# One list of steps, sums on GpSimd and a weighed minus plane in a fused attention and dense layer

## The chip, the cores and the metric

The kernel runs on one core of one Trainium2 chip. A core has TensorE (matrix products, results in PSUM), VectorE (DVE in the profile), ScalarE (ACT), GpSimd (POOL), SyncE (SP, which here only issues DMAs) and 16 DMA engines. The metric is the device time of one execution in microseconds. PSUM has eight banks of 128 partitions x 512 fp32 numbers.

## The reference

The input x has 2048 rows of 512 numbers. A layernorm gives xn, and the result is x plus an attention branch plus a dense branch, both fed by xn, all in bf16:

```python
def _A_ref(x, wqkv, w_phi, wo):                    # H = 32 heads of Dh = 16
    q, k, v = ...                                  # x @ wqkv, split into heads
    pq = jnp.einsum("bhsd,hdf->bhsf", q, w_phi)
    pk = jnp.einsum("bhsd,hdf->bhsf", k, w_phi)
    phi_q = jnp.concatenate([softmax(pq), softmax(-pq)], axis=-1)
    phi_k = jnp.concatenate([softmax(pk), softmax(-pk)], axis=-1)
    kv = jnp.einsum("bhsf,bhsd->bhfd", phi_k, v)
    z  = jnp.einsum("bhsf->bhf", phi_k)
    num = jnp.einsum("bhqf,bhfd->bhqd", phi_q, kv)
    den = jnp.einsum("bhqf,bhf->bhq", phi_q, z)[..., None] + 1e-6
    return (num / den, heads joined) @ wo

def _B_ref(x, w1, b1, w2):                         # 512 -> 1792 -> 512
    h = jnp.einsum("bsd,df->bsf", x, w1) + b1
    return jnp.einsum("bsf,fd->bsd", mish(h), w2)

return x + _A_ref(xn, ...) + _B_ref(xn, ...)
```

## The kernel before, in words

The 2048 rows are 16 tiles of 128, four tiles to a group. The softmax features are worked on in eight steps s: s = 0 to 3 are the keys of groups 0 to 3, s = 4 to 7 the queries. The key weights and w_phi are multiplied into one matrix `wkp` at the start (`fold`), the query weights into `wqp` later.

**Keys.** `logits` is a product of xnT (xn transposed) with `wkp`, copied out of PSUM to `p_sb`. `extremes` makes two planes per group on VectorE: logits minus their maximum over the 16 features of a head, and minimum minus logits, by a tree of maxima or minima (L234, L240) and a subtraction (L245). `exponentials` raises both on ScalarE, `normalise` (L277 sum, L287 reciprocal, L288 copy, L292 product) makes softmaxes of them on VectorE, and `accumulate` multiplies with the values (`value`, in `vext` with a column of ones), summing kv and z over all 16 tiles in `pkv` (L304). `mask_kv` keeps each head's own block, as `kvm`.

**Queries.** Here the exponentials are not normalised. Each tile of them is transposed by a DMA (`turn`, into `qT`), and `attend` multiplies it with `kvm` in 32 products of 32 rows and 36 columns, four of which lie side by side in TensorE's rows (`tile_position`, L350). Plus and minus planes, each with its own numerator, denominator and softmax sum, come out apart in `pnd`; ScalarE copies them to `ds` and `nm` (L359, L362), and `combine` joins them on VectorE (L379 to L403), a DMA transposes the result into `ob`, and `project_out` adds the product with `wo` to the same PSUM bank, `po`, as the dense branch's second layer (`second_layer`, L422; L431). `residual` adds x, `store` issues the stores.

**Dense.** `hidden` makes 56 units of 128 features x 512 rows (4 products of 128x512 each, L194), `activate` applies Mish on ScalarE (L207).

**Layernorm.** `ln_stats` (L133, L135) runs on VectorE, the root on GpSimd; `ln_apply` on VectorE for group 1 and on GpSimd for groups 2 and 3 (L145). Group 0 is transposed on TensorE, the others by DMAs (`ln_turn_dma`, L163).

Nothing is scheduled by a tool: each engine works through its instructions in the order in which the program issues them, and waits where data or a buffer is missing. All DMAs but a few stand in SyncE's queue. The program first issues x (three loads of SyncE's, L450, L456, L459), the key weights, `wv` (L457) and w1 (L458); w2 (L556) and `wo` (L557) are issued behind the first two transposes of `xnT`. The order of the rest is written out by hand: a loop over s for the keys, in which the hidden units fill TensorE's time, then a straight list of calls for the queries.

Of the kernel before, what the change touches and what calls it, by code (L numbers as in the profile page):

```python
# [14 lines left out]
AX = mybir.AxisListType  # L15


@with_exitstack
def kernel(
# [41 lines left out]
    ps = ctx.enter_context(tc.tile_pool(name="ps", bufs=4, space=PSUM))  # L61
    upper = ExitStack()
    px = upper.enter_context(tc.tile_pool(name="px", bufs=1, space=PSUM))
    turns = [cycle([px, ps, ps, ps, ps])]

    def bank(name, dtype=FP32, pool=None):
        pool = pool or next(turns[0])
        return pool.tile([P, 512], dtype, name=name, tag="mm")

    def three_banks(name, bufs):  # L70
        stack = ExitStack()
        return stack, stack.enter_context(tc.tile_pool(name=name, bufs=bufs, space=PSUM))
# [4 lines left out]
    kvm = persist.tile([P, 8, 36], BF16, name="kvm")  # L77
# [17 lines left out]
    vext = [vpool.tile([P, TPG, 4, 4, 36], BF16, name=f"vext{i}") for i in range(2)]  # L95
# [11 lines left out]
    def fold(wT, dst, dve, kts=range(KT)):  # L107

        for kt in kts:
            pf = bank("pfold")  # L110
            for j in range(4):
                nc.tensor.matmul(  # L112
                    pf[:, j * P : (j + 1) * P],
                    lhsT=wT[:, j, kt * P : (kt + 1) * P],
                    rhs=Wbd[:, j, :],
                    start=True,
                    stop=True,
                )
            copy = nc.vector.tensor_copy if kt in dve else nc.scalar.copy
            copy(  # L120
                dst[:, kt, :].rearrange("p (b a c) -> p a b c", b=8, a=2),
                pf[:].rearrange("p (a b c) -> p a b c", a=2, b=8),
            )

    def ln_stats(t0, n, between=None):

        stats = lnp.tile([P, TPG, nc.vector.BN_STATS_DIM], FP32, name="stats")
        mv = lnp.tile([P, TPG, nc.vector.BN_AGGR_DIM], FP32, name="mv")
        rstd = lnp.tile([P, TPG], FP32, name="rstd")
        for i in range(n):  # L130
            if i == 1 and between is not None:
                between()
            nc.vector.bn_stats(stats[:, i, :], x_sb[:, t0 + i, :])  # L133
        for i in range(n):
            nc.vector.bn_aggr(mv[:, i, :], stats[:, i, :])  # L135
        nc.gpsimd.tensor_scalar(
            out=rstd[:, 0:n], in0=mv[:, 0:n, 1], scalar1=1e-5, scalar2=None, op0=ALU.add
        )
        nc.gpsimd.tensor_tensor(out=rstd[:, 0:n], in0=rstd[:, 0:n], in1=mhalf[:, 0:n], op=ALU.pow)
        return mv, rstd  # L140

    def ln_apply(t0, n, mv, rstd, xn, at):
        engine = nc.gpsimd if t0 > TPG else nc.vector
        for i in range(n):
            engine.tensor_scalar(  # L145
                out=xn[:, at + i, :],
                in0=x_sb[:, t0 + i, :],
                scalar1=mv[:, i, 0:1],
                scalar2=rstd[:, i : i + 1],
                op0=ALU.subtract,  # L150
                op1=ALU.mult,
            )

    def ln_turn_pe(t, xn, i, copy):
        ptr = bank("ptr", BF16)
        for kt in range(KT):
            nc.tensor.transpose(  # L157
                ptr[:, kt * P : (kt + 1) * P], xn[:, i, kt * P : (kt + 1) * P], ident[:]
            )
        copy(xnT[:, t, :, :], ptr[:].rearrange("p (k c) -> p k c", k=KT))  # L160

    def ln_turn_dma(t, xn, i):
        nc.sync.dma_start_transpose(  # L163
            out=xnT[:, t : t + 2, :, :].rearrange("p t k c -> p (t k) c"),
            in_=xn[:, i : i + 2, :].rearrange("p t c -> p (t c)"),
        )
# [12 lines left out]
    def value(t, copy):  # L179
        pv = project(wv, t)  # L180
        copy(
            vext[(t // TPG) % 2][:, t % TPG, :, :, 0:32].rearrange("p j r c -> p (j r) c"),
            pv.rearrange("p (j c) -> p j c", j=16),
        )

    units = iter([(g, f) for g in range(NG) for f in range(FT)])

    def hidden(n, pool=None, late=None):

        for _ in range(n):  # L190
            g, f = next(units)
            ph = bank("ph", FP32, pool)
            for kt in range(KT):
                nc.tensor.matmul(  # L194
                    ph[:],
                    lhsT=w1_sb[:, kt, f * P : (f + 1) * P],
                    rhs=xnT[:, g * TPG : (g + 1) * TPG, kt, :],
                    start=(kt == 0),
                    stop=(kt == KT - 1),
                )  # L200
            if late is None:
                activate(g, f, ph)
            else:
                late.append((g, f, ph))
# [7 lines left out]
    p_of, e_of, qT_of = {}, {}, {}  # L212

    def logits(s, i, copy):
        if i == 0:
            p_of[s] = smx.tile(
                [P, TPG, 512], BF16, name="p_sb" if s < 7 else "p_last", bufs=1
            )
        pp = project(wkp if s < NG else wqp, (s % NG) * TPG + i)
        copy(p_of[s][:, i, :], pp)  # L220

    def extremes(s, between=None, halves=(slice(0, TPG),)):

        if s not in e_of:
            e_of[s] = epool.tile([P, TPG, 16, 2, 32], BF16, name="e")
        for q in halves:
            n = q.stop - q.start
            e = e_of[s][:, q]
            pv = p_of[s][:, q, :].rearrange("p t (c e) -> p (t c) e", e=16)
            for pl, op in enumerate((ALU.max, ALU.min)):  # L230
                src = pv
                for half in (8, 4, 2):
                    m = smx.tile([P, 128, half], BF16, name=f"m{half}", bufs=1)[:, 0 : n * 32, :]
                    nc.vector.tensor_tensor(  # L234
                        out=m, in0=src[:, :, 0:half], in1=src[:, :, half : 2 * half], op=op
                    )
                    src = m

                m = smx.tile([P, 128, 1, 2], BF16, name="m1", bufs=1)[:, 0 : n * 32]
                nc.vector.tensor_tensor(out=m[:, :, 0, :], in0=src, in1=src[:, :, ::-1], op=op)  # L240
                if pl == 0 and between is not None:
                    between()
                mb = m.rearrange("p (b h) u o -> p b h u o", h=2).to_broadcast([P, n * 16, 2, 8, 2])
                p5 = pv.rearrange("p (b h) (e o) -> p b h e o", h=2, o=2)
                nc.vector.tensor_tensor(  # L245
                    out=e[:, :, :, pl, :].rearrange("p t b (h e o) -> p (t b) h e o", h=2, o=2),
                    in0=p5 if pl == 0 else mb,
                    in1=mb if pl == 0 else p5,
                    op=ALU.subtract,
                )  # L250

    def exponentials(s, ks=(0, 1)):
        for k in ks:
            m = 1 if s >= NG or (s > 1 and k == 0) else 2
            for i in range(2 * k, 2 * k + 2, m):
                v = e_of[s][:, i : i + m].rearrange("p t b l c -> p (t b l c)")
                nc.scalar.activation(v, v, ACT.Exp)  # L257
                if s >= NG:
                    turn(s, k, i)

    def turn(s, k, i):

        h = 2 * (s - NG) + k
        if i == 2 * k:
            qT_of[h] = epool.tile([P, 2, 8, P], BF16, name="qT", bufs=3)
        nc.sync.dma_start_transpose(
            out=qT_of[h][:, i - 2 * k, :, :],
            in_=e_of[s][:, i].rearrange("p b l c -> p (b l c)"),
        )

    def normalise(s, k, between=None):

        v = e_of[s][:, 2 * k : 2 * k + 2].rearrange("p t b l c -> p (t b l c)")
        t = smx.tile([P, 128], FP32, name="s")
        n = 64 if s > 1 and k == 0 else 128
        for c in range(0, 128, n):
            nc.vector.reduce_sum(  # L277
                t[:, c : c + n],
                v[:, 16 * c : 16 * c + 16 * n].rearrange("p (c e) -> p c e", e=16),
                axis=AX.X,  # L280
            )
        if between is not None:
            between()
        r = smx.tile([P, 128], BF16, name="r")
        r2 = smx.tile([P, 128, 2], BF16, name="r2")
        with nc.allow_low_precision("the softmaxes are bf16"):
            nc.vector.reciprocal(r[:], t[:])  # L287
# [8 lines left out]
    kv_of = {}  # L296

    def accumulate(g, pk):
        if g == 0:
            kv_of[0] = pk.tile([P, 8, 128], FP32, name="pkv", tag="kv")  # L300
        e = e_of.pop(g)
        for b in range(8):
            for i in range(TPG):
                nc.tensor.matmul(  # L304
                    kv_of[0][:, b, 0:66],
# [429 lines left out]
```

## Time and profile before

| | |
|---|---|
| time, median of 3 runs | 178.31 us (178.26 to 178.38) |
| span of the profiled execution, first to last instruction | 176.1 us; its own time isn't given apart from the three runs', and 2.2 us of their median lie around the span |
| granted TensorE clock | 1.000 |
| TensorE's last product ends | 172.2 us |
| GpSimd, largest row | L145 apply, 16.6 us in 8 instructions of 2.08 us |
| ScalarE, table loads | 13 of 1.28 us |

In the profile PE is TensorE's products, PEld its weight loads, SPq SyncE's issues of DMAs; a row of the timeline gives start, length, engine, line, operation, output <- input and count. The lengths of single products overlap (379 ns each at a rate of 216 ns), so rates are taken from the chain.

### The profile page before, as it was taken

The numbers are of one execution on the slowest core, as the hardware profiler recorded it, in microseconds if no ns is written. First come the engines' busy times: TensorE is split into PE (matmuls) and PEld (weight loads), VectorE is DVE, ScalarE is ACT, GpSimd is POOL, SyncE is SP. The second block draws the span as 40 slices with busy tenths as digits, with TensorE's granted clock in tenths as the row PEclk, the third lists the DMA queues.
The fourth block names the chain that finished last, engine by engine and source line by source line (L and its number), as shares of the span: only waits on it lengthen the run. The fifth ranks groups of instructions, "written<-read, shape, count | busy, mean of one in ns | idle before, by whom it ended". The sixth has DMA issues, their size and how long they took to land.

```text
span 176.1 us, 3589 instructions
## 1 busy us (share of the span) xinstructions
PE 171.1 (97%) x1422; PEld 81.6 (46%) x1422; DVE 154.1 (88%) x308; ACT 125.4 (71%) x176; POOL 28.5 (16%) x40
## 2 busy tenths in 40 slices
PE   6899999999999999999999999999999999999993
PEld 2444444454444545554454444444444444444561
DVE  0989999999999999999999979798789978789953
ACT  3667999999998899989996699489223863544200
POOL 4203039700799400000000000000000000000000
PEclk9999999999999999999999999999999999999999
DMA  5998895330023600000000942919945098394434
GB/s 139 272 416 314 131 348 177 60 61 4 0 49 69 124 0 0 0 0 4 0 0 0 179 92 56 100 29 133 229 119 93 3 170 99 91 121 123 65 89 149
DMA packets 44557, 18.08 MB, mean 103 GB/s; under 512 B 36988, under 2 KB 44028, under 8 KB 44540
## 3 DMA queue, kind: packets, MB, share of 16 engines
q1 hardware_dynamic: 43568, 17.50, 46.6%
q10 hardware_dynamic: 972, 0.35, 0.7%
q8 instruction: 11, 0.18, 0.4%
q14 instruction: 6, 0.05, 0.1%
HBM read 6.84 MB, written 2.10 MB: 51 GB/s over the span
## 4 chain that ended last, share of the span: by engine, by line
PE 93%; DVE 3%; DMA 2%; DVEq 0%; issue 0%
PE po L422 28%; PE ph L194 28%; PE pproj L173 22%; PE po L431 7%; PE pnd L350 3%; PE pkv L304 2%; DMA x_sb<-in_A_x_dram 2%; PE pwide L173 1%; DVE stats L499 1%; DVE x_sb L439 1%; PE pfold L112 1%; DVE xn L512 0%; DVE wkp L120 0%; DVE mv L503 0%; PE ptr L157 0%; DVEq L730 0%
## 5 line engine op out<-in xcount | busy, mean ns | idle before, releaser
L422 PE MATMUL po<-w_sb,acts 128*128 128x512 bf16 (+1 forms) x238 | 51.0, 367 | 0.0
L194 PE MATMUL ph<-xnT,w_sb 128*128 128x512 bf16 x224 | 49.5, 379 | 0.0
L207 ACT ACTIVATE acts<-ph,b1f 128x512 bf16<-128x512 f32 x56 | 34.6, 704 | 2.0 <-PE ph L194 1.9
L257 ACT ACTIVATE e<-e 128x1024 bf16<-128x1024 bf16 (+1 forms) x26 | 31.0, 1250 | 4.6 <-DVE e L245 4.6
L194 PEld LDWEIGHTS <-w_sb 128*128 128x128 bf16 x224 | 21.9, 98 | 26.4 <-issue 0.3
L422 PEld LDWEIGHTS <-acts 128*128 128x128 bf16 x238 | 22.2, 98 | 22.5
L173 PEld LDWEIGHTS <-xnT 128*128 128x128 bf16 x192 | 18.2, 98 | 22.0 <-issue 1.2
L277 DVE TENSOR_REDUCE s<-e 128x128 f32<-128x2048 bf16 (+1 forms) x10 | 18.3, 1850 | 0.0
L359 ACT COPY ds<-pnd 128x128 f32<-128x128 f32 x16 | 4.2, 265 | 17.4 <-PE pnd L350 15.8
L145 POOL TENSOR_SCALAR xn<-x_sb,mv,rstd 128x512 bf16<-128x512 bf16 x8 | 16.6, 2079 | 0.2
L439 DVE TENSOR_TENSOR x_sb<-po,x_sb 128x512 bf16<-128x512 f32 (+1 forms) x17 | 11.0, 658 | 6.2 <-PE po L431 6.2
L431 PE MATMUL po<-wqk,ob 128*128 128x512 bf16 (+1 forms) x68 | 15.0, 367 | 0.0
L173 PE MATMUL pproj<-wv,xnT 128*128 128x512 bf16 x64 | 15.0, 379 | 0.0
L234 DVE TENSOR_TENSOR m<-m 128x256 bf16<-128x256 bf16 (+2 forms) x44 | 13.4, 305 | 1.5
L173 PE MATMUL pproj<-wqk,xnT 128*128 128x512 bf16 x64 | 14.5, 379 | 0.0
L220 ACT CAST p_sb<-pproj 128x512 bf16<-128x512 f32 x20 | 10.7, 585 | 3.4 <-PE pproj L173 1.8
L173 PE MATMUL pproj<-wkp,xnT 128*128 128x512 bf16 x52 | 12.6, 379 | 0.2
L292 DVE TENSOR_TENSOR e<-e,r 128x2048 bf16<-128x2048 bf16 x8 | 10.7, 1337 | 0.3
L234 DVE TENSOR_TENSOR m<-p_sb 128x1024 bf16<-128x1024 bf16 (+1 forms) x18 | 10.2, 566 | 0.0
L431 PEld LDWEIGHTS <-ob 128*128 128x128 bf16 x68 | 6.5, 98 | 6.8 <-DMA ob<-ob 0.3
L245 DVE TENSOR_TENSOR e<-m,p_sb 128x2048 bf16<-128x2048 bf16 (+1 forms) x9 | 8.9, 988 | 0.3
L245 DVE TENSOR_TENSOR e<-p_sb,m 128x2048 bf16<-128x2048 bf16 (+1 forms) x9 | 8.9, 989 | 0.3
(73 smaller groups left out, 175.1 us busy)
## 6 DMA issues: line engine op xcount, KB each, us to landing
w_sb<-in_B_w_dram SPq DMA_DIRECT2D x2, 1792.0 KB, 8.4
out_dram<-x_sb SPq DMA_DIRECT2D x15, 128.0 KB, 1.9
x_sb<-in_A_x_dram SPq DMA_DIRECT2D x1, 1024.0 KB, 11.2
x_sb<-in_A_x_dram SPq DMA_DIRECT2D x1, 512.0 KB, 4.3
wv<-in_A_wqkv_dram SPq DMA_DIRECT2D x1, 512.0 KB, 5.0
wqk<-in_A_wo_dram SPq DMA_DIRECT2D x1, 512.0 KB
x_sb<-in_A_x_dram SPq DMA_DIRECT2D x1, 256.0 KB, 3.2
x_sb<-in_A_x_dram ACTq DMA_DIRECT2D x1, 256.0 KB, 3.5
```

What stands on the lines that cost most here:

```text
L145: engine.tensor_scalar(out=xn[:, at + i, :], in0=x_sb[:, t0 + i, :], scalar1=mv[:, i, 0:1], scalar2=rstd[:, i : i + 1], op0=ALU.subtract, ...
L173: nc.tensor.matmul(pp, lhsT=xnT[:, t, kt, :], rhs=w[:, kt, :], start=(kt == 0), stop=(kt == KT - 1),)
L194: nc.tensor.matmul(ph[:], lhsT=w1_sb[:, kt, f * P : (f + 1) * P], rhs=xnT[:, g * TPG : (g + 1) * TPG, kt, :], start=(kt == 0), stop=(kt == ...
L207: nc.scalar.activation(acts[:, f, g * 512 : (g + 1) * 512], ph[:], ACT.Mish, bias=b1f[:, f : f + 1])
L220: copy(p_of[s][:, i, :], pp)
L234: nc.vector.tensor_tensor(out=m, in0=src[:, :, 0:half], in1=src[:, :, half : 2 * half], op=op)
L245: nc.vector.tensor_tensor(out=e[:, :, :, pl, :].rearrange("p t b (h e o) -> p (t b) h e o", h=2, o=2), in0=p5 if pl == 0 else mb, in1=mb i ...
L257: nc.scalar.activation(v, v, ACT.Exp)
L277: nc.vector.reduce_sum(t[:, c : c + n], v[:, 16 * c : 16 * c + 16 * n].rearrange("p (c e) -> p c e", e=16), axis=AX.X,)
L422: nc.tensor.matmul(po[:, c], lhsT=acts[:, f, t * P : (t + 1) * P], rhs=w2_sb[:, f, c], start=(f == 0), stop=False,)
L431: nc.tensor.matmul(po[:, c], lhsT=oT_of[h][:, t % 2 * 4 + j, :], rhs=wo_sb[:, j, c], start=False, stop=(j == 3),)
L439: nc.vector.tensor_tensor(out=y, in0=po[:, c], in1=y, op=ALU.add)
```

## The change

Five things change together.

1. *Order.* Behind the head (group 0's layernorm, the fold of the keys, the logits of step 0) all work is one text, `PLAN`, of named steps that `step` issues one after the other. `unit_g_f` is a hidden unit's products and `unit=_g_f` its Mish; `logits_s_i` and `logits=_s_i_e`, `value`, `fold` likewise, with the last number choosing ScalarE (0) or VectorE (1) for the copy; for `apply` and `sums` it chooses VectorE (0) or GpSimd (1). `plane_s_p` is one plane of a group, `plane_s_p_q` of half a group, `exp_s_i` the exponential of one tile, `add_g_i` one tile's part of `accumulate`, `second_t_q` half of a second layer.
2. *Sums.* The softmax sums of a tile (64 sums of 16) are a step of their own. 26 of the 32 are on GpSimd, as four additions that halve the width; 6 are a reduction on VectorE.
3. *Queries.* `weigh` multiplies the minus plane by the ratio of the plus sum to the minus sum before it is transposed, so that both planes share one denominator.
4. *Products with kv.* `kvm` has both planes' rows in one block-diagonal matrix of 68 columns (64 numerators, 4 denominators), and `attend` is 8 products of 128 rows. `divide` reads the result in PSUM, in place of the copies and `combine`.
5. *Buffers and loads.* PSUM has six common banks and two for `pkv`, later for `pnd` (one buffer). The loads of w2 and `wo` are issued ahead of the whole list.

```diff
+PLAN = """
+spread_6 spread_4 spread_5 value_0 spread_7 value_3 gather_1 value=_0_0 plane_0_0 root_1 value_2
+value=_3_0 value_1 apply_7_1 unit_0_7 apply_4_0 unit_0_10 unit=_0_7 apply_5_0 spread_11 apply_6_1
+turned_4 unit_0_8 unit=_0_10 spread_14 value=_2_0 unit_0_6 spread_10 value=_1_0 spread_8 unit_0_2
+unit=_0_8 masks turned_6 plane_0_1 unit=_0_6 unit_0_12 unit=_0_2 logits_1_0 unit=_0_12 value_5
+spread_9 logits_1_1 exp_0_1 gather_2 value_7 spread_12 root_2 logits=_1_0_0 spread_13 exp_0_2
+logits_1_2 logits=_1_1_1 logits_1_3 exp_0_3 sums_0_1_1 spread_15 unit_0_1 apply_10_0 value=_5_0
+apply_8_0 value=_7_0 apply_9_0 unit_1_5 gather_3 exp_0_0 apply_11_0 unit_0_9 logits=_1_3_1
+sums_0_2_1 turned_10 logits=_1_2_0 unit_1_0 plane_1_0 turned_8 unit_1_1 unit=_0_1 unit_1_3
+sums_0_0_1 unit=_1_5 unit=_1_1 unit_0_0 unit=_0_9 plane_1_1 unit_1_8 unit=_0_0 wq unit_0_3 unit=_1_0
+sums_0_3_1 unit=_1_8 unit_2_10 unit=_1_3 logits_2_1 unit=_2_10 normal_0_0 unit=_0_3 logits_2_3
+root_3 logits=_2_1_0 value_6 logits=_2_3_0 logits_2_2 normal_0_1 logits_2_0 exp_1_3 add_0_0 value_4
+exp_1_2 sums_1_3_1 value=_6_1 fold_1 exp_1_0 unit_0_13 apply_12_0 apply_14_0 unit_1_9 exp_1_1
+apply_15_0 logits=_2_2_1 add_0_2 sums_1_2_1 logits=_2_0_0 fold=_1_1 add_0_3 add_0_1 value=_4_0
+unit_1_10 apply_13_0 plane_2_0 turned_12 unit_1_7 unit_0_4 unit=_0_13 turned_14 sums_1_0_1 unit=_1_9
+unit_2_2 unit=_1_10 normal_1_1 unit_1_4 unit=_0_4 unit=_1_7 unit_0_11 sums_1_1_1 unit=_2_2 fold_2
+unit=_1_4 value_11 unit=_0_11 plane_2_1 fold_0 unit_2_8 fold=_0_0 value=_11_0 unit_1_6 unit=_2_8
+logits_3_2 fold=_2_0 unit=_1_6 normal_1_0 add_1_2 logits_3_0 logits=_3_2_0 add_1_3 value_8 exp_2_2
+logits_3_3 logits=_3_0_1 value=_8_1 logits_3_1 exp_2_1 logits=_3_3_1 add_1_1 logits=_3_1_1 add_1_0
+sums_2_1_1 fold_3 value_10 fold=_3_0 exp_2_3 value_9 value=_10_1 plane_3_0 exp_2_0 value_15
+sums_2_3_1 unit_1_11 value=_15_0 value=_9_0 unit_1_12 unit_2_1 plane_3_1 sums_2_2_1 unit=_1_11
+unit_1_2 logits_4_3 unit=_1_2 unit=_2_1 logits_4_0 unit=_1_12 sums_2_0_1 normal_2_1 logits_4_2
+logits_4_1 exp_3_1 value_13 logits=_4_3_0 normal_2_0 value_12 logits=_4_0_0 value_14 logits=_4_2_0
+logits=_4_1_0 logits_5_1 exp_3_3 value=_13_1 logits_5_0 exp_3_0 sums_3_3_1 value=_12_1 add_2_3
+value=_14_1 add_2_0 logits=_5_0_0 add_2_2 add_2_1 exp_3_2 unit_2_7 plane_4_0_1 unit_2_3
+logits=_5_1_0 sums_3_1_1 unit_0_5 plane_4_0_0 unit_3_4 unit=_2_7 unit=_0_5 unit_2_5 unit=_3_4
+sums_3_2_1 plane_4_1_0 unit_2_13 unit=_2_3 unit_3_11 unit_3_5 plane_4_1_1 unit=_3_11 sums_3_0_1
+unit=_2_5 unit_2_12 unit=_3_5 logits_5_2 normal_3_1 unit=_2_13 unit=_2_12 logits_6_0 logits_6_3
+unit_3_1 exp_4_1 logits=_5_2_1 normal_3_0 unit_3_3 logits=_6_0_0 sums_4_1_1 exp_4_0 logits_6_2
+logits=_6_3_0 add_3_3 add_3_2 unit_1_13 sums_4_0_0 unit_3_8 unit=_3_1 weigh_0 add_3_0 unit=_3_3
+unit_2_6 logits=_6_2_0 add_3_1 unit=_1_13 unit_3_9 turn_0_1 plane_5_0_0 unit=_3_8 logits_5_3
+unit=_3_9 turn_0_0 unit_2_9 logits=_5_3_0 unit=_2_6 plane_5_0_1 unit_3_0 unit=_2_9 unit_3_13
+unit=_3_0 unit_3_2 kv unit=_3_13 unit_2_4 plane_5_1_0 unit_3_6 exp_4_2 logits_6_1 exp_4_3 attend_0_0
+second_0_0 divide_0_0 exp_5_0 sums_4_3_1 sums_4_2_0 out_0_0 attend_0_1 second_0_1 divide_0_1
+unit=_3_2 sums_5_0_1 unit=_2_4 unit_3_12 weigh_1 out_0_1 unit=_3_6 unit_3_10 plane_5_1_1 turn_1_0
+second_1_0 exp_5_1 turn_1_1 project_0 sums_5_1_0 exp_5_3 logits_7_1 exp_5_2 residual_0 second_1_1
+weigh_2 logits=_6_1_0 sums_5_2_1 attend_1_0 logits_7_3 turn_2_1 divide_1_0 unit=_3_10 project_1
+unit=_3_12 turn_2_0 sums_5_3_1 attend_1_1 residual_1 unit_2_11 plane_6_0_0 store_0 unit_2_0
+unit=_2_11 out_1_0 logits=_7_1_0 logits_7_2 logits=_7_3_1 second_2_0 divide_1_1 weigh_3 logits_7_0
+attend_2_0 second_2_1 plane_6_1_0 turn_3_1 unit_3_7 store_1 divide_2_0 turn_3_0 second_3_0 unit=_3_7
+logits=_7_2_0 plane_6_0_1 out_1_1 unit=_2_0 attend_2_1 project_2 logits=_7_0_0 out_2_0 second_3_1
+residual_2 divide_2_1 exp_6_0 second_4_0 plane_7_0_0 out_2_1 exp_6_1 project_3 sums_6_1_1 sums_6_0_0
+second_5_0 plane_7_1_0 attend_3_0 second_7_0 divide_3_0 exp_7_1 second_4_1 weigh_4 exp_7_0
+sums_7_1_1 attend_3_1 project_4 plane_6_1_1 turn_4_1 second_7_1 turn_4_0 residual_3 exp_6_3
+second_5_1 sums_7_0_0 out_3_0 exp_6_2 sums_6_3_1 second_8_0 divide_3_1 sums_6_2_0 out_3_1 second_6_0
+weigh_5 attend_4_0 project_5 turn_5_0 second_9_0 divide_4_0 weigh_6 store_2 second_6_1 turn_5_1
+turn_6_1 attend_4_1 second_8_1 divide_4_1 out_4_0 residual_4 project_6 plane_7_0_1 out_4_1
+attend_5_0 second_9_1 turn_6_0 plane_7_1_1 project_7 store_4 second_14_0 divide_5_0 exp_7_2
+project_8 residual_5 exp_7_3 residual_7 attend_5_1 project_9 sums_7_3_1 divide_5_1 second_10_0
+residual_8 out_5_1 residual_6 second_11_0 out_5_0 sums_7_2_1 store_8 attend_6_0 second_10_1
+divide_6_0 residual_9 attend_6_1 second_12_0 weigh_7 project_10 divide_6_1 turn_7_0 second_14_1
+residual_10 turn_7_1 second_11_1 store_5 store_7 out_6_0 second_12_1 out_6_1 project_11 attend_7_0
+store_6 residual_11 second_13_0 divide_7_0 project_12 out_7_0 second_13_1 residual_12 attend_7_1
+project_13 divide_7_1 second_15_0 out_7_1 project_14 store_11 store_10 second_15_1 residual_14
+store_12 store_9 residual_13 store_13 project_15 store_14 store_3 residual_15 store_15
+"""
...
-    kvm = persist.tile([P, 8, 36], BF16, name="kvm")
+    kvm = persist.tile([P, 8, 68], BF16, name="kvm")
...
+    def sums(s, i, engine):
+        k = i // 2
...
+        out = sum_of[s, k][:, i % 2, :]
+        part = e_of[s][:, i].rearrange("p b l (h e) -> p (b l h) e", h=2)
+        if engine is nc.vector:
+            nc.vector.reduce_sum(out, part, axis=AX.X)
+            return
+        for n in (8, 4, 2, 1):
+            to = smx.tile([P, 64, n], FP32, name=f"t{n}", bufs=1) if n > 1 else out[:, :, None]
+            nc.gpsimd.tensor_tensor(
+                out=to[:], in0=part[:, :, 0:n], in1=part[:, :, n : 2 * n], op=ALU.add
+            )
+            part = to
+
+    def weigh(h):
...
+        nc.vector.reciprocal(rm[:], sums[:, :, 1, :])
+        nc.vector.tensor_tensor(out=r2[:], in0=sums[:, :, 0, :, None]..., in1=rm[:, :, :, None]..., op=ALU.mult)
...
+        nc.vector.tensor_tensor(out=minus, in0=minus, in1=r2[:, :, :, None, :]..., op=ALU.mult)
...
     def normalise(s, k):
-            nc.vector.reduce_sum(...)
+        t = sum_of.pop((s, k))
...
     def attend(h, i):
-        pnd = later[0].tile([P, 4, 512], FP32, name="pnd", tag="nd")
+        pnd = later[0].tile([P, 2, 512], FP32, name="pnd", tag="nd")
         for b in range(8):
-            for r in range(4):
-                rows = slice(32 * r, 32 * r + 32)
-                nc.tensor.matmul(
-                    pnd[:, r % 2 * 2 + r // 2, 36 * b : 36 * b + 36],
-                    lhsT=qT_of[h][rows, i, b, :], rhs=kvm[rows, b, :],
-                    start=True, stop=True, tile_position=(32 * r, 0),
-                )
-        nc.scalar.copy(ds..., a[:, :, :, 32:36])
-        nc.scalar.copy(nm..., a[:, :, :, 0:32])
+            nc.tensor.matmul(
+                pnd[:, b // 4, 68 * (b % 4) : 68 * (b % 4) + 68],
+                lhsT=qT_of[h][:, i, b, :], rhs=kvm[:, b, :], start=True, stop=True,
+            )
...
-    def combine(h, parts=(slice(0, 2),), amid=None):
...
+    def divide(h, i):
...
+        nc.vector.reciprocal(r[:], nd[:, :, :, 64:68])
+        nc.vector.tensor_tensor(out=o_t..., in0=nd[:, :, :, 0:64]..., in1=r..., op=ALU.mult)
...
     for i in range(2, TPG):
-        logits(0, i, act)
...
-    extremes(0, lambda: normal(TPG, st, xn))
+        logits_copy(0, i, project(wkp, i), act)
     nc.sync.dma_start(w2_sb[:], w2_v[:, :, :])
     nc.sync.dma_start(wo_sb, wo_v[:, :, :])
...
+    for name in PLAN.split():
+        step(name)
```

## The prediction

> **What bounds the kernel now.** I read the page's busy times first, then the chain of work in order of time, then the timeline of VectorE, GpSimd and SyncE where the change puts new work.
>
> ```profile
> PE 171.1 (97%) x1422; PEld 81.6 (46%) x1422; DVE 154.1 (88%) x308; ACT 125.4 (71%) x176; POOL 28.5 (16%) x40
> ```
>
> TensorE is busy all the time, VectorE nearly so. The chain shows at what rate TensorE works:
>
> ```profile
> 38.74 0.99 PE pkv L304 x32
> 39.74 6.91 PE pproj L173 x32
> ...
> 95.45 3.02 PE po L422 x14
> ...
> 107.07 0.31 PE pnd L350 x32
> 107.38 3.13 PE po L422 x14
> ...
> 172.20 0.02 issue
> ```
>
> (start us, length, what, how many.) From 8.8 to 172.2 us the chain is TensorE alone: 0.216 us for a 128x512 product (6.91/32, 3.02/14), 0.031 for a 66-column one, 0.31 for an `attend` of 32 row-tiled ones. The 14 products behind an `attend` take 3.13 where the undisturbed 14 take 3.02. So less work on ScalarE or VectorE brings nothing by itself; the time is TensorE's work plus its gaps, and before has none.
>
> ```profile
> 6.46 0.51 SPq L459 DMA_DIRECT2D x_sb<-in_A_x_dram  x1
> 16.39 3.62 SPq L163 DMA_TRANSPOSE xnT<-xn  x2
> 20.06 0.57 SPq L556 DMA_DIRECT2D w_sb<-in_B_w_dram  x1
> ...
> 27.00:28.00 1.00, 1.00 1.08 382
> 28.00:29.00 1.00, 1.00 0.52 180
> ```
>
> (SyncE's issues, then two stretches with DMA share and GB/s.) By issue plus time to landing (L456 4.74 + 4.3, L457 5.36 + 5.0, L458 5.90 + 8.9, L459 6.46 + 11.2) the loads land in the order of issue: x 4:8 at 9.0, `wv` 10.4, w1 14.8, x 8:16 17.7 us. The first transpose of `xnT` landed at 16.4 + 3.6 = 20.0, the second at 22.0, w2 and `wo` behind them, flowing until about 28.5.
>
> ```profile
> 25.91 8.28 POOL L145 TENSOR_SCALAR xn<-x_sb,mv,rstd 128x512 bf16<-128x512 bf16 x4
> 28.18 1.67 DVE L292 TENSOR_TENSOR e<-e,r 128x2048 bf16<-128x2048 bf16 x1
> 33.39 1.23 DVE L292 TENSOR_TENSOR e<-e,r 128x2048 bf16<-128x2048 bf16 x1
> ...
> 56.86 1.23 DVE L245 TENSOR_TENSOR e<-p_sb,m 128x2048 bf16<-128x2048 bf16 x1
> 56.96 1.21 POOL L331 COPY kvm<-block 32x16 bf16<-32x16 bf16 x1
> ```
>
> GpSimd and VectorE hold each other up. A 16-element copy that takes 0.21 us elsewhere took 1.21 and ended with VectorE's TENSOR_TENSOR; and of two equal TENSOR_TENSORs the one met by a fresh GpSimd instruction (the second of the four starts at 27.98) took 0.44 more, as if held until 28.62, 0.64 us into GpSimd's 2.07.
>
> **TensorE's work.** `attend` becomes 8 full products of 68 columns, by the `pkv` row 8 x 0.031 = 0.25 instead of 0.31: 16 x 0.06 = -0.9 us. Of the 0.11 lost behind row tiles (between 0 and 16 x 0.11 = 1.8), I take the 12 places where the chain shows it: -1.3. All else on TensorE is the same count. Without gaps: 178.3 - 2.2 = 176.1 us. The profiled span is 176.1; 2.2 us lie around it, and I work on the median, since span + 2.2 equals it.
>
> **ScalarE.** Loses 16 x (1.02 + 0.26) = 20.5 us of copies from `pnd`; per-tile exponentials between Mish units make 17 table loads of 13 (+5.1). It isn't the bound before (125 of 176) nor after; nothing.
>
> **The loads, moved.** w2 and `wo` are issued right behind x 8:16, ahead of `turned_4` and `turned_6`; nothing in front of them on SyncE waits. They are 2.36 MB: 6.5 us by the stretch 22.0 to 28.5, 5.8 at the 400 GB/s of 8 to 16 us. Behind x 8:16's landing at 17.7 that gives 23.5 to 24.2, and the first transpose landed 2.3 us behind its predecessor: 24.8 to 26.5, I take 26.0, the second 28.0. If transposes are not held by loads, it is 17.4 (second `apply` ends) + 3.6 = 21.0. TensorE stands at `logits_1_0` after 4 value and 6 hidden units: 12.5 (the first value product's start, as before) + 10 x 0.863 (four products of 0.216) = 21.1. So it stops for 4.9 us (3.7 to 5.4; 0 if not held); behind it in the list wait `value_5`, the other logits, and VectorE's copy `logits=_1_1_1`, which holds VectorE 3.6 us. Before, units cover this and w2 comes after.
>
> **VectorE up to the queries.** The list lets TensorE reach `add_3_0` at 86.8: 12.5 + 81 groups x 0.863 + 14 adds x 0.248 + 4 folds x 0.222. Ahead of it VectorE must finish `normal_3_0`: 12 statistics x 0.62, 3 gathers x 0.36, 10 applies x 0.36, 8 full planes x 2.95, 4 half planes x 1.82, 14 PSUM copies x 0.64, 8 normals x 2.45 = 71.6 us from 10.9 on, the start of tile 4's statistics as before: 82.5. (Durations are starts to starts in VectorE's timeline, where neighbours overlap a little.) That is with the sums (18.3 us in L277's row) gone, and leaves 4.3 us of room.
>
> **The sums on GpSimd.** 26 of 32 go there, 16 of them before `normal_3_0`. One is 4 adds of 512, 256, 128 and 64 outputs. The 512-wide row is L476's 1.15 us; tiny ones take 0.2; a line through both gives 1.15 + 0.68 + 0.44 + 0.32 = 2.6 us. GpSimd alone has room for that (16 x 2.6 = 42 in 55 us). The price is what VectorE loses. Between 25 and 82.5 us, 37 of its 57 us (planes 25, normals' last two steps 12) are of the kind held up above: a share of 0.65. What each sum takes from such work: 0 if the one row misleads, 0.44 if only the widest add costs, 2.6 if GpSimd holds VectorE for its whole length. Nearest is the 0.64 seen for 512 elements; scaled by width 0.64 + 0.32 + 0.16 + 0.08 = 1.2. Loss: 16 x 0.65 x 1.2 = 12.5 us. VectorE then ends `normal_3_0` at 82.5 + 3.6 + 12.5 = 98.6 and TensorE is 98.6 - 86.8 = 11.8 us late; the 4.9 above are contained in it. 176.1 + 11.8 = 187.9.
>
> **The query half.** Combining went from 33 us to 16 divides (0.22 + 0.69) and 8 `weigh`s (1.55); VectorE has 68 us of work in TensorE's last 83, and 10 more sums cost at most 10 x 0.65 x 1.2 = 8: covered. `weigh` now stands between exponentials and `turn`; the list has 9 us from `weigh_0` to `attend_0_0` for a transpose that lands in 4.1. At the end `out_7_1` has `project_13`, `second_15`, `project_14`, 4.9 us, for a divide (0.9) and a landing (2.4); without that cover about 1 us. One wait is new: `pnd` has one buffer and VectorE's `divide` now reads it, so the next `attend`, with all of TensorE's queue behind it, waits for `divide` where it waited for ScalarE's copies (1.3 us). The list puts at least seven products (1.5 us) between two `attend`s; a `divide` that finds VectorE in a half plane comes up to 1.8 + 0.9 - 1.5 = 1.2 us late, at worst 15 times. With some 15 us of room on VectorE there I take nothing. The stores stand last on SyncE as before.
>
> **Rivals.** *Only the transposes are late*: the lock costs 0.44 a sum, 4.6 us in all; VectorE ends at 90.7, before TensorE's 91.7, and the time is 176.1 + 4.9 = 181.0. For it: VectorE lost just 0.44 to a 2.07 us instruction, and many instructions of that window ran undisturbed. Against: that instruction reads one tensor, an add reads two, and small adds follow at once. *Faster*: neither holds; transposes pass the loads and VectorE keeps its 4.3 us of room (lock loss under about 4 us): 176.1, decided by the landing of the first `xnT` transpose before 21.1. For it: no row shows a transpose queued behind megabytes. Against: the first transpose took SyncE 2.27 us instead of 1.25 while x 8:16 was landing. *GpSimd holds VectorE for its whole length*: 16 x 0.65 x 2.6 = 27 us, VectorE at 113.1, 26.3 late, 202.4.
>
> The Trainium skill says this in "SBUF — State Buffer", section "Who interferes with whom": whichever of a GpSimd instruction that reads SBUF and a VectorE instruction with two SBUF inputs starts first holds the shared port for all of its length. The trace agrees for VectorE (1.21 us behind a 1.23 us instruction) and differs for GpSimd (0.64 of 2.07).
>
> **How the numbers follow.** Forecast 187.9, call it 188 (0.46): its own range is 182.7 to 196.2, a sum costing 0.7 to 2.0 (what an add that reads twice as much may hold). Late transposes alone 0.23, faster 0.20, whole-length hold 0.09; 0.02 that it comes out even. The range goes from 176 to 196: it leaves out the lower half of the faster case, the whole-length case and the top of the forecast's own, some 2 in 10. A measurement tells about 0.2%, 0.4 us, from no change. Faster 0.20, same 0.02, slower 0.78.
>
> **What would show it.** A gap on TensorE at about 21 us with a DMA of `xnT` as releaser; adds on GpSimd longer than 1.15 us and VectorE's 128x256 steps well over 0.29; gaps before `pkv` released by VectorE, growing to 12 us by the last; then none. Wrong: `xnT` landing before 21 us, unchanged VectorE rows beside the adds, or the largest gaps behind 100 us.

## The result, and the profile after

The changed kernel takes 196.98 us (median of four, 196.44 to 198.04) against 178.28: 1.106 times the time, interval 1.1025 to 1.1088. The forecast was 188 and its range ended at 196. The direction and the two causes came as forecast; 9 us of the size were missing. The profiled execution took 196.97 us with a span of 195.3. The engines' row of the page (busy us, share, instructions), then TensorE's clock in 40 slices:

```profile
PE 174.8 (90%) x1038; PEld 83.6 (43%) x1038; DVE 163.8 (84%) x295; ACT 111.1 (57%) x151; POOL 95.5 (49%) x135
PEclk9999969999999999789987999999999999999999
```

TensorE has 3.7 us more busy time than before although its products are the same or fewer: some of them ran at a lower clock (the slices with 6 to 8). GpSimd went from 28.5 to 95.5 us, VectorE from 154.1 to 163.8, though the change took the 18.3 us of the key half's sums off it.

The longest waits that TensorE now has, from its timeline (start, length, instructions, and in brackets how long it stood before them and who released it):

```profile
26.00 1.72 PE L236 MATMUL pproj<-wkp,xnT 128*128 128x512 bf16 x4 [4.75 <-DMA xnT<-xn]
...
65.31 0.69 PE L375 MATMUL pkv<-vext,e 128*128 128x66 bf16 x16 [1.50 <-DVE e L362]
...
80.21 1.29 PE L236 MATMUL pproj<-wv,xnT 128*128 128x512 bf16 x4 [2.76 <-ACT p L271]
...
101.86 1.06 PE L375 MATMUL pkv<-vext,e 128*128 128x66 bf16 x16 [3.25 <-DVE e L362]
...
128.55 0.41 PE L412 MATMUL pnd<-kvm,qT 128*128 128x68 bf16 x8 [1.82 <-DVE ob L428]
```

So the first stop ends at 26.0, with the landing of the first `xnT` transpose, 8.4 us behind its issue (3.1 is the median in the kernel before). The forecast was 26.0 out of 24.8 to 26.5, and the tenth is luck: in other runs with the same early loads the first product behind the stop starts between 25.3 and 26.2. Then TensorE waits for VectorE's normal steps (L362), once for a ScalarE copy that stands behind an exponential which itself waits for VectorE (80.21), and, in the query half, for `divide` (L428).

Beside each other, VectorE and GpSimd at 86 us, as timelines of the two:

```profile
86.56 1.08 DVE L289 TENSOR_TENSOR m<-m 128x128 bf16<-128x128 bf16 x1
87.74 1.17 DVE L292 TENSOR_TENSOR e<-p,m 128x1024 bf16<-128x1024 bf16 x1
...
86.40 1.15 POOL L315 TENSOR_TENSOR t<-e 128x512 f32<-128x512 bf16 x1
```

The 128x128 step of VectorE takes 0.226 us in the kernel before. Here it starts 0.16 us into GpSimd's add of 512 and ends at 87.64, 0.09 behind the add: it was held for the whole rest of the add, not until 0.64 us into it as the prediction's row had it. This holding is called the lock below. What was held and what was not shows in VectorE's rows by form (busy us, mean ns), first in the kernel before, then in the changed one:

```profile
L287 DVE RECIPROCAL r<-s 128x128 bf16<-128x128 f32 x8 | 7.6, 953 | 0.3
...
L245 DVE TENSOR_TENSOR e<-p_sb,m 128x2048 bf16<-128x2048 bf16 x5 | 6.1, 1226 | 0.1
...
L277 DVE TENSOR_REDUCE s<-e 128x64 f32<-128x1024 bf16 x4 | 4.7, 1214 | 0.0
...
L240 DVE TENSOR_TENSOR m<-m 128x256 bf16<-128x256 bf16 x10 | 2.9, 292 | 0.3
...
L240 DVE TENSOR_TENSOR m<-m 128x128 bf16<-128x128 bf16 x12 | 2.7, 226 | 0.4
```

```profile
L428 DVE TENSOR_TENSOR ob<-pnd,r 128x512 bf16<-128x512 f32 x16 | 11.1, 691 | 0.7
...
L357 DVE RECIPROCAL r<-sums 128x128 bf16<-128x128 f32 x8 | 7.6, 945 | 0.9 <-POOL sums L315 0.9
...
L210 DVE TENSOR_SCALAR xn<-x_sb,mv,rstd 128x512 bf16<-128x512 bf16 x14 | 7.3, 556 | 0.1
L311 DVE TENSOR_REDUCE sums<-e 128x64 f32<-128x1024 bf16 x6 | 7.3, 1209 | 0.0
...
L292 DVE TENSOR_TENSOR e<-p,m 128x2048 bf16<-128x2048 bf16 x4 | 6.6, 1656 | 0.2
...
L289 DVE TENSOR_TENSOR m<-m 128x256 bf16<-128x256 bf16 x8 | 4.6, 574 | 0.3
```

Steps with two tensor inputs in SBUF are longer. The reciprocal, the reduction and `divide`'s product (0.692 us in a run without the adds) are not. The Trainium skill says in "SBUF — State Buffer", section "Who interferes with whom", that a VectorE instruction with at most one SBUF input doesn't contend with GpSimd outside the two-port modes, which copies and scalar steps can enter, and that one with two SBUF inputs contends with a GpSimd instruction that reads SBUF. The rows agree, on the exception too: the scalar step of the layernorm (L210) has one tensor input and takes 0.556 us, against 0.427 in a run without the adds, and a copy of 0.29 us (L358) took 1.00 at 99.07, behind an add that had started at 98.77. Whether these two ran in such a mode, no row shows.

### The profile page after: what moved, and what is told of

Its sections match the earlier page's. It is cut to its first block, busy times and chain, and to the rows that moved or that the text cites. A ratio compares the mean times of both kernels' runs of the same rounds, so it can differ in the third digit from the quotient of the medians.

```text
span 195.3 us, 2885 instructions
## 1 busy us (share of the span) xinstructions
PE 174.8 (90%) x1038; PEld 83.6 (43%) x1038; DVE 163.8 (84%) x295; ACT 111.1 (57%) x151; POOL 95.5 (49%) x135
## 4 chain that ended last, share of the span: by engine, by line
PE 36%; DVE 33%; DMA 12%; POOL 7%; issue 4%; ACT 3%; SPq 3%; DVEq 0%; ACTq 0%; POOLq 0%
PE po L448 13%; PE ph L251 10%; DVE m L284 8%; PE pproj L236 7%; POOL t L315 6%; DMA x_sb<-in_A_x_dram 6%; DVE e L292 5%; DMA xnT<-xn 4%; PE po L457 4%; DVE ob L428 2%; DVE sums L311 2%; DVE xn L210 2%; DVE m L289 2%; DVE e L362 2%; DMA ob<-ob 2%
## 5 line engine op out<-in xcount | busy, mean ns | idle before, releaser
L315 POOL TENSOR_TENSOR t<-e 128x512 f32<-128x512 bf16 x26 | 33.0, 1270 | 61.1 <-ACT e L301 61.1
L301 ACT ACTIVATE e<-e 128x1024 bf16<-128x1024 bf16 x32 | 32.3, 1052 | 21.4 <-DVE e L292 16.4
L315 POOL TENSOR_TENSOR t<-t 128x256 f32<-128x256 f32 (+1 forms) x52 | 37.4, 720 | 4.1
L251 PEld LDWEIGHTS <-w_sb 128*128 128x128 bf16 x224 | 21.8, 99 | 26.2 <-issue 2.3
L284 DVE TENSOR_TENSOR m<-m 128x256 bf16<-128x256 bf16 (+2 forms) x48 | 18.8, 392 | 1.6
L271 ACT CAST p<-pproj 128x512 bf16<-128x512 f32 x24 | 13.6, 582 | 6.3 <-PE pproj L236 6.3
L284 DVE TENSOR_TENSOR m<-p 128x512 bf16<-128x512 bf16 (+1 forms) x24 | 14.2, 592 | 0.1
L292 DVE TENSOR_TENSOR e<-p,m 128x1024 bf16<-128x1024 bf16 (+1 forms) x12 | 13.7, 1141 | 0.6
L180 DVE BATCH_NORM_STATS2 stats<-x_sb 128x6 f32<-128x512 bf16 x16 | 10.2, 678 | 4.0 <-DMA x_sb<-in_A_x_dram 3.9
L428 DVE TENSOR_TENSOR ob<-pnd,r 128x512 bf16<-128x512 f32 x16 | 11.1, 691 | 0.7
L292 DVE TENSOR_TENSOR e<-m,p 128x1024 bf16<-128x1024 bf16 (+1 forms) x12 | 10.7, 892 | 0.4
```

The costliest lines, as they stand in the source:

```text
L251: nc.tensor.matmul(ph[:], lhsT=w1_sb[:, kt, f * P : (f + 1) * P], rhs=xnT[:, g * TPG : (g + 1) * TPG, kt, :], start=(kt == 0), stop=(kt == ...
L284: nc.vector.tensor_tensor(out=m, in0=src[:, :, 0:half], in1=src[:, :, half : 2 * half], op=op)
L292: nc.vector.tensor_tensor(out=e[:, :, :, pl, :].rearrange("p t b (h e o) -> p (t b) h e o", h=2, o=2), in0=p5 if pl == 0 else mb, in1=mb i ...
L315: nc.gpsimd.tensor_tensor(out=to[:], in0=part[:, :, 0:n], in1=part[:, :, n : 2 * n], op=ALU.add)
L428: nc.vector.tensor_tensor(out=o_t.rearrange("p (u v g d) -> p u v g d", u=2, v=4, g=4), in0=nd[:, :, :, 0:64].rearrange("p u v (g d) -> p ...
```

## The experiments

**The two causes, one at a time and together.** Three kernels: the loads of w2 and `wo` back behind the transposes; GpSimd's sums replaced by a memset; both. With the memset the softmax sums are left out.

```diff
-    nc.sync.dma_start(w2_sb[:], w2_v[:, :, :])      # ahead of the list
-    nc.sync.dma_start(wo_sb, wo_v[:, :, :])
+ ... masks turned_6 weights plane_0_1 ...           # the same two issues as a step
```

> The changed kernel with the loads of w2 and wo issued behind turned_6 again. Theory (VectorE's lateness is the lock plus the early stop): TensorE's stop of 4.75 us at 26.0 and the lower clock behind it go, VectorE's idle 5.4 us at logits=_1_1 goes too, normal_3_0 ends at 99.4 instead of 104.8, and the time is 197.0 - 5.4 = 191.6 (190 to 193). Rival (the stop is contained in the later lag whole, as the prediction took it): 197 within 1. Second rival (the late transposes are the whole loss): 176 to 178.

```diff
-        for n in (8, 4, 2, 1):                       # the four GpSimd adds
+        nc.gpsimd.memset(out, 16.0)
```

> The changed kernel with GpSimd's 26 sums left out: a memset of the 64 sums to 16 stands in the place of the four adds, so nothing of e is read there; the softmax sums are not computed. Theory: VectorE's rows go back to those of before (128x256 steps 0.29, 128x512 0.43, e<-m,p 2048 1.23), no wait of TensorE on VectorE is left in the key half, the stop at 26.0 with its clock (6.6 us) stays: 176.1 + 6.6 = 182.7 (181 to 185). Rival (the new order itself starves TensorE: exponentials ahead of ScalarE's copies, one buffer of pnd): over 190 with the same waits.

> Both edits: loads behind turned_6 and memsets for GpSimd's adds (26 softmax sums are left out). Theory: no early stop, no lock: the running sum without gaps, 176.1, and 178 at most, 0 to 1.2% under the kernel before. Rival (the order): over 183.

Measured: loads back 194.42 (ratio to before 1.0901, 1.0871 to 1.0931); no adds 182.30 (1.0221, 1.0205 to 1.0236); both 176.19 (0.9879, 0.9864 to 0.9893). Both edits together give the forecast's sum without gaps, 176.1, to 0.1 us, so the order of the list starves nobody by itself, and the two causes are all there is. By itself the early stop costs 182.30 - 176.19 = 6.1 us, and the adds 194.42 - 176.19 = 18.2. Together they cost 20.8: the stop adds 2.6 to the adds, so the run with the loads back fell between its theory (5.4) and the rival (0), outside the range of both.

Why, the stretch from 10.9 us to the end of `normal_3_0` shows, in the four kernels in the order changed, loads back, no adds, both (length of the stretch, then for each engine its busy time and instructions, clock, DMA share, GB/s):

```profile
10.90:104.80 93.90, 81.00 (x458) 37.71 (x457) 84.97 (x134) 73.32 (x103) 67.69 (x85) 0.95 0.28 73
10.90:102.20 91.30, 78.61 (x463) 36.97 (x461) 87.26 (x135) 73.92 (x103) 67.24 (x85) 0.99 0.27 77
10.90:91.50 80.60, 76.54 (x445) 36.20 (x444) 70.02 (x134) 69.62 (x98) 14.56 (x36) 0.96 0.30 85
10.90:86.00 75.10, 74.63 (x448) 35.79 (x448) 69.99 (x134) 69.65 (x98) 14.63 (x36) 1.00 0.33 92
```

VectorE does the same 134 instructions each time (135 where the cut falls otherwise). Without adds they take 70.0 us, with them 85.0: the adds take 15.0 us from it. GpSimd works on 17 sums in that stretch (of its 85 instructions 17 are other work, by the run with all sums on VectorE below, and 68 are adds, four a sum): the 16 of the keys and the first of the queries, which starts at 98.77. So a sum takes 0.88 us from VectorE. The rest of each stretch is VectorE's idle time: 5.1 us with neither, 10.6 with the stop, 8.9 with both, 4.0 with the adds alone. With the loads back VectorE has 4.9 us less idle time than in the changed kernel, and loses 87.3 - 70.0 = 17.3 us to the adds instead of 15.0, 1.02 a sum. In the changed kernel GpSimd's first sum (25.44 to 28.24) and the first add of its second had met nobody, since VectorE stood idle from 25.1 to 30.5; now they meet it. Half of what the stop gives back goes to the lock.

**The sums on VectorE**, in the order of the change, to see what a sum is worth there:

```diff
- ... sums_0_1_1 ... sums_0_2_1 ...                   # last digit 1: GpSimd
+ ... sums_0_1_0 ... sums_0_2_0 ...                   # all 32 as VectorE reductions
```

> The changed kernel with all 32 sums as VectorE reductions (1.21 us each by the row of the six that are there already), GpSimd adds none; loads early as in the change. Theory (a sum on GpSimd takes 1.0 us from VectorE): VectorE gets 16 x 1.21 = 19.4 in place of 16.0 lost and 0.9 waited for: normal_3_0 2.5 us later, 199.5 (197 to 202); VectorE's other rows as before. Rival (the adds cost VectorE little, and its long rows have another cause): the reductions come on top, 197 + 19 = 216. Second rival (a sum on GpSimd costs VectorE much more than the rows tell, by waits): under 193.

201.19 us (1.1287, 1.1269 to 1.1306): within the theory's range, at its upper end, and far from the 216 by which the adds would be nearly free. All of VectorE's two-input rows are back at their old lengths (the 128x256 step 292 ns). In the same stretch (10.9 us to the end of `normal_3_0`) VectorE is busy for 86.95 us, so sixteen reductions of 1.21 us, which overlap their neighbours a little, add 17.0 to the 70.0: 1.06 a sum. A sum that leaves VectorE frees it of 1.06 us and takes 0.88 back.

**The adds in the kernel before.** To part the lock from the new order, GpSimd adds whose results nobody reads were put behind the masks of the kernel before:

```diff
             masks()
+            adds(12)      # 12 x GpSimd tensor_tensor adds of 64 x 8, 4, 2, 1 outputs
```

> The kernel before, in its own order, with 12 sets of GpSimd adds (64 x 8, 4, 2, 1 outputs, two inputs in SBUF, nobody reads the results) queued behind the masks at 59 us; nothing waits for them. Theory: GpSimd's adds alone lengthen VectorE's two-input steps, the new order is not needed for it: some 10 sets before normal's end at 88.7 take 0.85 each, VectorE had 2.2 us of room there before the last add, so TensorE stops for some 6 to 7 us before pkv: 185 (183 to 188), with VectorE's 128x512 and 128x256 steps stretched and its reductions and reciprocals not. Rival: off TensorE's chain or no hold: 178 to 179.

186.22 us (1.0441, 1.0423 to 1.0459), 1.2 us over the theory's point and within its range. VectorE's rows in it:

```profile
L277 DVE TENSOR_REDUCE s<-e 128x128 f32<-128x2048 bf16 x6 | 13.6, 2270 | 0.0
L292 DVE TENSOR_TENSOR e<-e,r 128x2048 bf16<-128x2048 bf16 x8 | 12.6, 1570 | 0.3
...
L240 DVE TENSOR_TENSOR m<-m 128x256 bf16<-128x256 bf16 x10 | 5.5, 554 | 0.3
```

The reduction keeps its 2.27 us, the two-input steps go from 1.34 and 0.29 to 1.57 and 0.55 on the mean. The last normal step ends at 96.46 instead of 88.67: 7.8 us for ten sets (the four adds of a sum) and most of an eleventh, some 0.7 a set. TensorE stopped in another place than expected, once for a VectorE copy behind those steps (2.75 us at 84.78, and the next 8 products took 3.51 us instead of 1.89) and later for another copy and a transpose. Nothing waits for these adds: holding VectorE is all that they do, and the new order is not needed for it.

**One input instead of two on GpSimd.**

```diff
-            nc.gpsimd.tensor_tensor(out=to[:], in0=part[:, :, 0:n], in1=part[:, :, n : 2 * n], op=ALU.add)
+            nc.gpsimd.tensor_copy(to[:], part[:, :, 0:n])
```

> The changed kernel with each GpSimd add turned into a copy of its first input alone (same output, one SBUF input in place of two; the other half of each sum is left out). Theory: any GpSimd instruction that reads SBUF holds VectorE for its length, so VectorE's loss goes with GpSimd's busy time (1.0 us lost per 2.65 us before): with copies of about half the length 188 (185 to 192), rows of VectorE still stretched in proportion. Rival: only instructions with two inputs hold: VectorE's rows as in the kernel without adds, 182.3 within 1.

182.62 us (1.025, 1.0211 to 1.029), as without adds. But the time alone misleads, as the stretch up to `normal_3_0` shows:

```profile
10.90:94.40 83.50, 78.66 (x460) 37.15 (x459) 74.29 (x134) 71.78 (x100) 47.79 (x85) 0.96 0.31 82
```

VectorE's work there is 74.3 us, 4.3 over the 70.0 without adds, for 47.8 - 12.4 = 35.4 us of copies on GpSimd (12.4 is its other work there, by the run with all sums on VectorE): 0.12 us lost for each us, where the adds' 67.7 - 12.4 = 55.3 us cost 15.0, 0.27 each. The 4.3 us don't reach TensorE, whose timeline shows no wait for VectorE in that run. So neither theory came: a copy holds VectorE too, at half the rate of an add or a little less. A set of copies takes 1.6 us where it meets nobody (at 25.93) and 35.4 / 17 = 2.1 here, so GpSimd loses some 8 us to VectorE's 4.3; with the adds it is some 10 to VectorE's 15.0 (worked out below). The prediction's nearest row, a one-input TENSOR_SCALAR that held 0.64 of 2.07 us, is therefore no measure of an add. The section of the Trainium skill named above makes no difference between GpSimd instructions that read one tensor and two; these rows do. Whether it is the second input, the kind of instruction or what the instructions met was not parted.

**The clock.** The stop filled with products that nobody reads:

```diff
- ... unit=_0_2 logits_1_0 ...
+ ... unit=_0_2 warm logits_1_0 ...       # warm: 20 products wkp x wkp into an unused bank
```

> The changed kernel with 20 products (wkp by wkp into a bank that nobody reads) in TensorE's stop ahead of logits_1_0: 4.3 of the 4.75 us are filled, the transposes still land at 26.0. Theory of the clock: the granted clock stays at 1.0 behind the stop, the 12 products take 2.59 instead of 4.46 us, VectorE's logits=_1_1 comes some 1.3 to 1.9 us earlier and so does the end: 195.4 (195 to 196). Rival (the slow 12 products are due to something else, as w2 and wo still flowing): 12 products still 4.4 us, 197.0.

The clock behind the stop, changed kernel and then this one:

```profile
26.00:30.00 4.00, 4.00 (x11) 1.48 (x12) 0.00 (x0) 2.25 (x3) 2.64 (x5) 0.57 0.08 17
26.00:30.00 4.00, 3.98 (x19) 1.86 (x20) 1.17 (x2) 2.90 (x5) 3.63 (x6) 1.00 0.10 21
```

The clock stays at 1.00 instead of 0.57, 19 products fit where 11 did, and VectorE's `logits=_1_1` starts at 28.83 instead of 30.49. So the clock is settled as the cause of the slow products, and the rival is out: from 27 to 30 us no DMA moved anything in either run, and the clock of the changed kernel was still 0.50 to 0.59. But the time is 196.81 (196.61 to 197.82), not to be told from 196.98: of the 1.66 us VectorE still has 0.9 at `normal_3_0` (103.92 instead of 104.85), and no gain is left at the end.

**The query half.** Key sums as in the change, the ten GpSimd sums of the queries replaced by memsets (`if s >= NG`):

> The changed kernel with GpSimd's 10 query sums left out (memset to 16 in their place), the 16 key sums kept. Theory: TensorE's lag at add_3_0 stays (18.7 us by its list), only the waits of attend for divide behind 100 us go: 197.0 - 2.5 = 194.5 (193.5 to 195.5). Rival (the query half is covered, as the prediction took it): 197 within 0.5. Second rival (it cost more than these waits): under 192.5.

192.76 us (1.0807, 1.0792 to 1.0823): 4.2 us less. That is outside the theory's range (2.5 expected), just short of the second rival (4.5 and more), and clearly not the nothing of the prediction. No wait of TensorE behind 100.71 is left. 1.1 us of it lie ahead of that (`normal_3_0` ends at 103.73 instead of 104.85, since in the changed kernel the first query sum runs beside the last key steps: behind its adds a copy took 1.00 us and a product 1.63, here 0.32 and 1.23), 3.1 behind.

**Versions.** If VectorE's time is the limit, the sums have to become cheaper there. A tree of four adds over two tiles at once does in 0.68 + 0.43 + 0.29 + 0.29 = 1.69 us (its rows) what two reductions do in 2.42:

```diff
-            nc.vector.reduce_sum(out, part, axis=AX.X)          # 128x64 <- 128x1024, one tile
+            for n in (8, 4, 2, 1):                              # two tiles, bf16 partial sums
+                nc.vector.tensor_tensor(out=to, in0=part[:, :, 0:n], in1=part[:, :, n : 2 * n], op=ALU.add)
```

> A version: the changed kernel with the loads behind turned_6, and every sum on VectorE as a tree of four adds over two tiles at once (bf16 partial sums): 0.69 + 0.42 + 0.29 + 0.23 = 1.63 us a pair by VectorE's rows of these widths, 0.81 a tile instead of 1.21 by the reduction, and GpSimd idle. Theory: VectorE needs 71.6 + 8 x 1.63 = 84.6 us from 10.9 to normal_3_0: 95.5; TensorE 95.5 - 86.8 = 8.7 late: 185 (183 to 187). Rival (the sums need more, since waits on exponentials come with them): over 188.

187.84 us (1.0542, 1.051 to 1.0573): 2.8 over the point and just outside the theory's range, but short of the rival. `normal_3_0` ends at 97.9 instead of 95.5, by the same little gaps of VectorE that the prediction's sum lacks (below). The sums in themselves cost what was expected. Then the list was written anew, three times, with nothing else changed; most of VectorE's copies out of PSUM go to ScalarE:

> A version: the sums as VectorE trees and the loads behind turned_6 as in the run of the trees, with a new list: 12 of VectorE's 14 copies out of PSUM go to ScalarE (12 x 0.6 = 7 us off VectorE, which ScalarE, busy 111 of 187 us, has room for), and units, planes and logits stand in an order in which VectorE never waits long. Theory: VectorE then needs some 150 of 176 us, TensorE's stops shrink from 12 us to 1 to 3, and the time comes to 176.1 + 1 to 3: 178 (176.5 to 179.5), even with the kernel before or just under it. Rival (stops of some microseconds stay, since VectorE and TensorE must meet at each normal step): over 181.

> The same version with another list made in the same way (10 of the 14 copies on ScalarE, 47 units instead of 42 ahead of the last add of kv, where the list of the change has 44). Theory: 176.5 to 179.5 as well; the stop ahead of the last adds smaller, since more units cover it. Rival: over 181.

> A version: sums as VectorE trees, 11 of VectorE's 14 copies out of PSUM on ScalarE, and a third list that keeps the loads of w2 and wo behind both first transposes and keeps ScalarE's copies out from behind a row of exponentials, where the two lists before lost 5.7 us (the transposes behind the loads) and 3.2 us (a copy behind four exponentials). Theory: what is left is the running sum, 176.1, and waits for the transposes of ob of 1 to 3 us as in the second list: 178 (176.5 to 179.5), about even with the kernel before. Rival (VectorE, at 150 of 176 us, is late at some step in any list): over 181.

The first took 185.72 us (1.0422, 1.0399 to 1.0445), the second 183.27 (1.0267, 1.0235 to 1.0298): both expectations fell, each mainly by one wait near the start, not by VectorE's load (the second has 2.1 us of waits for the transposes of `ob` besides):

```profile
29.68 1.89 PE L236 MATMUL pproj<-wkp,xnT 128*128 128x512 bf16 x4 [5.67 <-DMA xnT<-xn]
```

```profile
25.33 0.54 PEld L236 LDWEIGHTS <-xnT 128*128 128x128 bf16 x4 [3.64 <-DMA xnT<-xn]
25.33 1.04 PE L236 MATMUL pproj<-wv,xnT 128*128 128x512 bf16 x4 [3.15 <-ACT e L301]
```

In the first the loads stood between the first two transposes, and the second landed late. In the second a value product stands still. Its row names an exponential of ScalarE, but the weight load that starts with it names the landing of a transpose, which was issued only at 22.12, behind two layernorm steps of GpSimd, and landed 3.2 us later; ScalarE's last copy out of PSUM ahead of it had ended at 23.43. So it was the transpose by these rows, and not, as the expectation of the third list says, a copy behind exponentials. The third list has neither wait and takes 178.15 us (177.72 to 178.34; ratio 0.9993, 0.9984 to 1.0002): even with the kernel before, as expected. Its longest wait of TensorE is 0.39 us. No version beat the kernel before; the 176.19 above leaves sums out.

## Why the prediction was wrong, point by point

The step that failed is the sum of VectorE's time up to `normal_3_0`, 71.6 + 3.6 + 12.5 us, with the query half, which was put at nothing. The mechanism is the one forecast: an early stop, and adds that hold VectorE. The sum had 5.3 us too little idle time and a lock 2.5 us too small; with steps that were put 1.6 too large it is 6.2 us short, and the query half cost 3.1. Term by term:

- **TensorE's work without gaps, 176.1**: right, 176.19 with both causes taken away. `attend` takes 0.26 us, and the 14 products behind it 3.02.
- **The stop behind the loads**: its place was right (first transpose at 26.0, stop 4.75 of the 4.9 forecast). Its size for VectorE was not: VectorE stood 5.37 us at `logits=_1_1`, not 3.6, because the products behind the stop were counted at 0.216 us each; the 12 of them took 4.29 us from start to start instead of 2.59, since the clock had fallen. Filling the stop gave VectorE 1.66 us of this back and the end time nothing, so the clock alone is not what was missing. And "contained" held only in part: 2.6 us of the stop are in the end time.
- **VectorE up to `normal_3_0`, 71.6 us**: its steps are right (70.0 us busy), but the sum held no idle time, and even with neither cause there are 5.1 us: waits of 0.3 to 0.9 for ScalarE's copies, a value product and x 8:16, and little gaps between instructions. So 75.1 us, and `normal_3_0` at 86.0 instead of 82.5; the room of 4.3 us against TensorE's 86.8 was 0.8.
- **A sum on GpSimd**: 2.6 us undisturbed, as forecast. It lasts 55.3 / 17 = 3.25 where VectorE holds it up in turn.
- **What the sums take from VectorE**: 12.5 forecast, 15.0 measured in the changed kernel, 17.3 when VectorE isn't idle. A sum takes 0.88 to 1.02; 0.65 x 1.2 = 0.78 was scaled from one row of a one-input instruction behind which VectorE went on after 0.64 of 2.07 us. One sum more than the 16 counted falls into the stretch. The whole-length rival (27 us) was too high although VectorE was held to the end of the add in the pair shown: it charged VectorE alone. GpSimd's 17 sums took 55.3 us instead of 17 x 2.64 = 44.9, so it lost some 10 itself, and 15.0 + 10.4 = 25.4 (with the loads back 17.3 + 9.9 = 27.2) is near the rival's 27. This split is an estimate from these sums, not followed meeting by meeting.
- **The sum**: 71.6 + 3.6 + 12.5 = 87.7 us from 10.9 to `normal_3_0` was forecast, 70.0 + 8.9 + 15.0 = 93.9 measured: idle time 5.3 too small, the lock 2.5 too small, the steps 1.6 too large, 6.2 in all.
- **The query half at nothing**: wrong by 3.1 us. The cover of "some 15 us of room" was an average; `divide` came late where it met adds and planes, and TensorE's whole queue stood behind the next `attend` (1.82 us at 128.55). The prediction had priced this wait at up to 1.2 us a time and then dropped it.
- **The signs named**: the stop at 21 us, the longer adds and the 128x256 steps came. The gaps before `pkv` did not grow to 12 us but came to 1.50 and 3.25. TensorE is 18.6 us late at `add_3_0` (105.44 instead of 86.8): its waits up to there make 12.9, and most of the rest is products at the lower clock.

187.9 + 6.2 + 3.1 = 197.2, against 196.98 measured. The case of late transposes alone (181.0) came out as 182.30 once the adds were gone, with a stop of 4.06 us and slower products behind it; the faster case (176.1) needs both causes away; the whole-length hold (202.4) overlooks that GpSimd pays a part of it.

## What to carry to other kernels

Work that is moved to GpSimd is not off VectorE while both read SBUF: here a sum took 1.06 us of VectorE's time with it and 0.88 came back, mostly as longer two-input steps, in rows that the change never touched, so look at those first. Sum a co-critical engine with its idle time, not only with its steps, and price a stop of TensorE with the lower clock behind it. When two causes each hide part of the other, only removing both shows what each is worth.

## What the runs showed of the hardware that was not expected

The clock of TensorE falls after stops shorter than the 4.75 us one. In the changed kernel a stop of 2.76 us, and in the run without query sums one of 2.18, were followed by half speed (stretches of the changed kernel behind 80.2, then of the other run in, behind and well behind its stop):

```profile
82.00:84.00 2.00, 2.00 (x6) 0.75 (x5) 1.86 (x4) 1.52 (x2) 1.35 (x1) 0.50 0.00 0
84.00:86.00 2.00, 2.00 (x38) 1.39 (x37) 1.97 (x5) 1.26 (x2) 1.84 (x3) 0.94 0.00 0
```

```profile
98.50:100.70 2.20, 0.03 (x1) 0.00 (x0) 2.06 (x4) 2.18 (x5) 0.15 (x1) 1.00 0.00 0
100.70:102.00 1.30, 1.29 (x18) 1.02 (x19) 1.30 (x2) 1.29 (x2) 0.00 (x0) 0.50 0.00 0
105.00:108.00 3.00, 3.00 (x22) 1.52 (x21) 2.72 (x8) 1.28 (x3) 0.24 (x2) 1.00 0.05 11
```

Stops of 1.50 us (at 65.31) and 1.82 us (at 128.55) left it at 1.00. The Trainium skill, "TensorE: Matmul & The Clock Gate", section "Part 1: The HAM clock gate", tells of a fall to half speed after an idle window of about 3.4 us, and of full speed after as long a busy one. Half speed and the 3 to 4 us until it is back agree (0.50 at 82 to 84, 0.94 from 84 on); the length of the stop does not, since 2.18 us were enough here.
